# A head dealt out anew: decay tables made row by row, and jobs moved between VectorE, ScalarE and GpSimd

## The chip, the cores and the metric

The kernel runs on one core of a Trainium2 chip. The metric is the device time of one execution in microseconds (us). Engines are named as in the profile: PE is TensorE (PEld its weight loads), DVE is VectorE, ACT is ScalarE, POOL is GpSimd, SP is SyncE, which here only issues transfers.

## What is computed

A block of a network on 2048 tokens of 640 channels, all in float32. First a state-space convolution between a layer norm and a residual, then a gated product of two matrices between another layer norm and a residual; shift, scale and gate of both come from one small vector `c`.

```python
mod = (silu(c) @ w_mod).reshape(1, 6, 1, -1)
sa, ca, ga, sb, cb, gb = ...                         # six rows of 640
h = layernorm(x) * (1 + ca) + sa
# convolution: per channel d, kernel K[d, l] = Re sum_n C[d,n] * exp(dt*A[d,n]*l) * dt*B[d,n], 192 states, 2048 taps
x = x + ga * (irfft(rfft(h, 4096) * rfft(K, 4096))[:2048] + h * Dskip)
h = layernorm(x) * (1 + cb) + sb
x = x + gb * (((h @ w_gate) * (h @ w_up)) @ w_down)  # 640 -> 1536 -> 640
```

## The kernel before

**Stages.** The first part, called the head here, makes the convolution's kernel and does the convolution; the last part is the gated product, in which TensorE multiplies weights and activations split in a rounded and a residual half.

**The head.** The 640 channels are five blocks `db` of 128; each block is two halves `hf`, each half four steps `n`, so 40 steps in all. The kernel's powers exp(dt*A*l) are split in a phase (sine and cosine) and a decay. Long ones are products of short tables: an index l is made of a low part (8 values) and a high part (row). For each step POOL writes three outer products with `outer` (L649): the phase table `Ph` (`mk_ph`, 128x1536 int32), the decay `EQ` (`mk_eq`, 128x1536) and the decay `EP` (`mk_ep`, 128x768), the last two from a low table (`LQ`, `LP`) and a high one (`RH`). ACT makes sine and cosine of `Ph` into PSUM (`k_sin`, `k_cos`, `u_abs`), DVE multiplies them with `EQ` and `EP` (`k_mul`, L731, six instructions of a step), TensorE contracts the products (`kg_ma`, `kg_mb`, L745 and L760). `EP` and `EQ` have two buffers each. `kg_out` and `u_k` bring the result through a copy into the first Fourier stage.

The low and high decay tables come from `u_seeds(db)`, a list of small steps. Its step `s_r` (L521, L523) multiplies a seed in PSUM by row factors held in a tile `mults`, 3 rows into `RL` and 11 into `RH`; `s_e` takes exponentials on ACT: seven into `LP` (scale 64 l), one over all of `RH`, one over three rows of `RL`. For later blocks, both halves go in one `s_e`; `s_r` runs once for each half.

Beside this the convolution's input goes through its own stages: layer norm (`u_stats`, `u_hm`), first transform (`u_pre`), second stage (`u_g`), product in the frequency domain (`u_c`), back (`u_d`). Each of them ends with copies from PSUM to SBUF, by the helper `act` (L135, all ACT instructions bear this line). The last block's product is done in two parts of each quarter.

**The order** is written out. `SCHED` gives to each step of each job a number, thousands for a tick and the rest for the order within a tick; `at` files the steps, `due` runs them tick by tick, 0 to 433. Negative numbers come before. Every engine takes its instructions in this order. `SLOT` gives to each allocation its buffer by a letter. Steps at tick 433 (`hd`) are the beginning of the gated product: sums of up and gate weights (`sums_u`, L1004 to L1007, on POOL), rounded and residual halves (`hilo`: ACT rounds, DVE subtracts, L992), transposes of tokens (`tokens2`). Ahead of that stand the layer norm of the first tokens (`u_ln`), their transposes (`u_first`, residual at L1149), and the first products (`u_gate`, L1162). `raw_u` issues the loads of gate and up weights of one column block.

Of the kernel before, what the change touches and what calls it, by code (L numbers as in the profile page):

```python
# [32 lines left out]
    ml=(13002, -99000, 0),  # L33
    mr=(((20003, 22002), (17004, 17008)), ((6001, 13000), (14000, 14001)), ((1, 1000), (1001, 3001))),
    st=((3000, 3004), (-90000, -89999), (-100997, 3005), (9000, 11005), (9001, 11004), (12001, 15001), (21001, 25006), (7000, 11000), (11001, 12002), (-100998, 11002), (20001, 22000), (19001, 20004), (9002, 11003), (-101000, -89998), (17003, 17009), (15000, 19002)),
    hm=((23000, 24000), (13001, 41000), (-100999, 20010), (30000, 32006), (40003, 40004), (-98999, 30004), (30001, 32002), (29000, 38001), (40002, 43000), (38002, 47000), (56004, 68000), (21002, 44003), (79003, 86004), (61002, 69000), (77000, 85000), (61000, 84002)),
    rstd=(17005, 30003),
    tab=(91000, 121003),
    fo=(22003, 31003, 31005, 35001),
    e0=(-87000,),  # L40
    mc=((31004, 39005, 40006, 43001, 52000), (34000, 53002, 60000, 62000, 69002), (58000, 91004, 92001)),
    q=((22004, 32000, 39001, 40005, 42006, 44000, 44001, 44002, 51000, 51001, 56001, 56002, 57000, 57002), (66002, 89000, 95003, 101000, 107000, 107001, 111000, 112000, 123000, 123003, 124001, 131000, 131003, 131004), (137001, 175000, 176001, 186009, 188001, 189001, 197003, 197004, 201000, 201001, 203002, 204001, 204002, 206001), (210002, 226000, 252005, 264003, 265002, 268001, 268002, 268003, 268005, 272001, 275000, 277000, 280002, 281001)),
# [10 lines left out]
    hl=((397000, 389000), (385000, 381000)),  # L53
    ln=((400000, 412000, 412003), (401000, 419002, 427000, 431007, 431010)),
    hd=(433000, 433017, 433028, 433035, 433027, 433001, 433005, 433003, 433008, 433009, 433010, 433012, 433007, 433024, 433021, 433016, 433026, 433014, 433018, 433013, 433004, 433023, 433022, 433034, 433036, 433025, 433019, 433031, 433039, 433011, 433002, 433006, 433029, 433033, 433038, 433030, 433040, 433037, 433020, 433032, 433042, 433041, 433015, 4880, 4880),
    ru=(409003, 367001),
    hg=(428002, 428003, 431004, 431005, 431012),
    rt=(410000,),
)

SLOT = dict(
    pa='23402424034345',
    Kt='abaaabaaabaabbabbaabbb',
    Ph='abababababababababababababababababababab',
    PtA='babababababaabbaaaabaabababababababababa',
    TV='ababbaabbaaaabababaabaabbababbbaba',
    W='abbaababaabaabbaababa',
    f16='abababab',
# [61 lines left out]
def tile_kernel(ctx: ExitStack, tc: tile.TileContext, I, out):  # L130
# [1240 lines left out]
    def s_one(k):  # L1371
        hilo(*part(1, k - 2), AT[TV1 + k])
# [252 lines left out]
```

## Time and profile before

| what | value |
|---|---|
| median of three runs | 962.99 us (959.34 to 963.2) |
| the profiled execution | 962.99 us, span 961.2 us |
| busy in the span: PE, DVE, ACT, POOL | 864.6, 760.1, 569.7, 567.8 us |
| granted TensorE clock, mean | 0.975 of full speed |
| POOL's last table of the head ends | 421.9 us |
| last matmul of the 40 steps ends | 433.5 us |

In the tables that follow, a row of the table by stage gives busy time and, in brackets, the number of instructions for each engine; a row of a group gives line, engine, operation, output and inputs, shape and count, then busy time and mean nanoseconds of one, then the engine's idle time just before and what ended it. A row of one line gives shortest, median and longest duration in nanoseconds. A row of waits gives who waited for whom: total, times, longest. A row of the chain or the timeline starts with the time from the span's start and the length.

### The profile page before, as it was taken

What the parts mean: (1) busy time and instruction counts of PE and PEld (TensorE: products, weight loads), DVE (VectorE), ACT (ScalarE), POOL (GpSimd) and SP (SyncE); (2) the same over time, 40 slices, a digit from 0 to 9 for tenths busy, and PEclk for the clock granted to TensorE, in tenths of its full rate; (3) what the DMA queues carried; (4) which work ended last, traced back from release to release, by engine and by line L of the source; (5) the groups of instructions that cost most, each with busy time, mean ns of one, the idle gap of its engine ahead of it and who ended that gap; (6) DMA issues with size and microseconds to landing.
All of it is one profiled execution on the core that took longest, in us unless ns stands there. A gap on an engine that the chain in (4) does not pass through costs nothing.

```text
span 961.2 us, 26424 instructions
## 1 busy us (share of the span) xinstructions
PE 864.6 (90%) x11070; PEld 715.9 (74%) x11070; DVE 760.1 (79%) x1328; ACT 569.7 (59%) x1022; POOL 567.8 (59%) x419
## 2 busy tenths in 40 slices
PE   2778876898798699989889999999999999999998
PEld 1565655676575467678567888899998888889998
DVE  8988678888989988897899877696677877688452
ACT  6889988887987888864773322235555322224330
POOL 5999999799799999950126767631031544451000
PEclk9977999899999889999999999999999999999999
DMA  9487565444565644558953454255536222212241
GB/s 301 152 267 263 150 217 191 134 132 126 145 181 147 186 130 144 161 175 266 254 168 89 130 192 139 80 192 164 193 137 219 84 83 82 83 55 83 83 165 55
DMA packets 141320, 148.94 MB, mean 155 GB/s; under 512 B 8208, under 2 KB 119568, under 8 KB 139792
## 3 DMA queue, kind: packets, MB, share of 16 engines
q1 hardware_dynamic: 139904, 145.80, 48.6%
q8 instruction: 87, 1.43, 0.6%
q10 hardware_dynamic: 1296, 1.44, 0.5%
q14 instruction: 33, 0.27, 0.1%
HBM read 108.36 MB, written 38.86 MB: 153 GB/s over the span
## 4 chain that ended last, share of the span: by engine, by line
PE 49%; DVE 4%; ACT 1%; DMA 1%; issue 1%; DVEq 0%; SPq 0%; ACTq 0%
PE pa L1028 28%; PE pa L1455 17%; PE psg L1028 1%; DMA wga<-B_w_gate 1%; DVE sl L992 1%; PE psg L1108 0%; PE psg L1455 0%; DVE a L1147 0%; PE psg L1162 0%; DVE xb L1468 0%; ACT wsgh L135 0%; PE psfa L887 0%; DVE f16a L873 0%; DVE f16a L874 0%; PE psfb L887 0%
## 5 line engine op out<-in xcount | busy, mean ns | idle before, releaser
L649 POOL TENSOR_TENSOR EQ<-LQ,RH 128x1536 f32<-128x1536 f32 x40 | 124.2, 3106 | 2.2 <-DVE QtB L731 2.1
L135 ACT ACTIVATE z<-pa 128x512 f32<-128x512 f32 x24 | 14.4, 599 | 168.0 <-PE pa L1028 115.0
L992 DVE TENSOR_TENSOR wsgl<-wga,wsgh 128x640 fp32r<-128x640 f32 x72 | 69.8, 973 | 45.6 <-ACT wsgh L135 45.6
L135 ACT ACTIVATE wsgh<-wga 128x640 fp32r<-128x640 f32 x72 | 52.3, 732 | 63.4 <-PE pa L1455 34.1
L1399 POOL TENSOR_TENSOR z<-z,s 128x512 f32<-128x512 f32 x24 | 34.2, 1423 | 88.4 <-DVE s L1398 88.4
L1004 POOL TENSOR_TENSOR tf<-wur,wgb 128x256 f32<-128x256 f32 x24 | 18.8, 784 | 97.0 <-DVE wtl L992 58.9
L649 POOL TENSOR_TENSOR EP<-LP,RH 128x768 f32<-128x768 f32 x40 | 65.7, 1651 | 11.8 <-DVE PtB L731 11.8
L1455 PE MATMUL pa<-wsgh,sh 128*128 128x384 f32 (+1 forms) x295 | 68.6, 311 | 0.0
L1455 PE MATMUL pa<-wsgl,sh 128*128 128x384 f32 (+1 forms) x295 | 68.2, 310 | 0.0
L1455 PE MATMUL pa<-wsgh,sl 128*128 128x384 f32 (+1 forms) x295 | 68.2, 310 | 0.0
L649 POOL TENSOR_TENSOR Pha<-LH,DH 128x1536 int32<-128x1536 int32 (+1 forms) x21 | 62.4, 2971 | 1.8 <-ACT tra L135 1.6
L649 POOL TENSOR_TENSOR Phb<-LH,DH 128x1536 int32<-128x1536 int32 x20 | 62.3, 3113 | 0.0
L992 DVE TENSOR_TENSOR wtl<-tf,wth 128x256 fp32r<-128x256 f32 (+1 forms) x72 | 58.8, 844 | 0.0
L731 DVE TENSOR_TENSOR QtA<-tra,EQ 128x1024 f32<-128x1024 f32 x44 | 51.9, 1215 | 7.7 <-ACT tra L135 4.8
L1397 DVE TENSOR_TENSOR s<-pa,s 128x512 f32<-128x512 f32 x24 | 16.6, 690 | 42.8 <-PE pa L1028 37.8
L731 DVE TENSOR_TENSOR QtA<-trb,EQ 128x1024 f32<-128x1024 f32 x36 | 42.7, 1217 | 9.7 <-ACT trb L135 5.5
L760 PE MATMUL kg<-QtB,PtB 64*32 64x64 f32 x2560 | 46.1, 222 | 4.7 <-issue 2.7
L760 PEld LDWEIGHTS kg<-QtB,PtB 64*32 64x32 f32 x2560 | 39.1, 110 | 12.5 <-issue 6.4
L1028 PE MATMUL pa<-sh,wtl 128*128 128x512 f32 x144 | 44.7, 391 | 0.8 <-DVE wtl L992 0.8
L1455 PEld LDWEIGHTS pa<-wsgh,sl 128*128 128x128 f32 x295 | 45.3, 188 | 0.0
L1455 PEld LDWEIGHTS pa<-wsgl,sh 128*128 128x128 f32 x295 | 45.3, 188 | 0.0
L1455 PEld LDWEIGHTS pa<-wsgh,sh 128*128 128x128 f32 x295 | 45.3, 188 | 0.0
(653 smaller groups left out, 2854.7 us busy)
## 6 DMA issues: line engine op xcount, KB each, us to landing
wga<-wdg SPq DMA_DIRECT2D x24, 640.0 KB, 4.2
wga<-B_w_gate SPq DMA_DIRECT2D x12, 640.0 KB, 5.8
wgb<-B_w_gate SPq DMA_DIRECT2D x24, 320.0 KB, 3.3
wur<-B_w_up SPq DMA_DIRECT2D x24, 320.0 KB, 4.0
xb<-x2d SPq DMA_DIRECT2D x6, 1280.0 KB, 7.1
t_ti<-w_mod SPq DMA_DIRECT2D x3, 1600.0 KB, 9.5
t_tw<-w_mod SPq DMA_DIRECT2D x3, 1600.0 KB, 9.8
WD<-Wa SPq DMA_DIRECT2D x8, 512.0 KB, 4.1
```

Source lines behind the costliest of these rows:

```text
L135: return S.activation(o, i, f, **kw)
L649: G.tensor_tensor(o.rearrange("p x (h l) -> p x h l", l=8), lo.unsqueeze(2).to_broadcast([P, rows, nh, 8]), hi.rearrange("p h x -> p x h") ...
L731: V.tensor_tensor(t, tr, e.unsqueeze(1).to_broadcast([P, 2, R, 32]), op=OP.mult)
L760: PE.matmul(kg[j * 32 : j * 32 + 32, dd, :], PtB[lo : lo + 64, c, r, :], QtB[lo : lo + 64, c, r, :], start=False, stop=dd == 7 and c == 1, ...
L992: V.tensor_tensor(lo, v, hi, op=OP.subtract)
L1004: G.tensor_tensor(t[:, 0:2], u[:, 0:2], g[:, 0:2], op=OP.subtract)
L1028: PE.matmul(ps, w[a][:, k], x[b][:, l], start=n == 0 and m == 0, stop=n == 2 and m == len(ks) - 1)
L1397: V.tensor_tensor(S67[i], ps, S6[i], op=OP.add)
L1399: G.tensor_tensor(ZT[i], ZT[i], S67[i], op=OP.add)
L1455: PE.matmul(ACC[tb][t][c], x[:, ts], w[:, cs], start=st, stop=f == NF - 1 and n == 2 and (one or t % 2 == 1))
```

## The change

1. `s_r` becomes a copy of the seed into row 0 of `RL`, for one half (`r`, `R`, in block 0) or both at once (`S`, later blocks). `mults` is gone. `s_e` makes every row of `RH` and `RL` by one ACT exponential with the row's factor as its scale: three rows, seven rows, three rows, beside the seven of `LP`. Row 3 of `RH`, which is always 1, is set once.
2. Copies, scalings and two-operand instructions of the head go through `put` and `tt`, which look up an engine in a new table `ENG` by the job's key; without an entry the engine is that of before.
3. `SCHED` and `SLOT` have new numbers throughout: every job of the head has a new place. Among them: the loads of the first gate and up weights (`ru`) move from tick 409 to 426, the load of the gate row (`w`, second entry) from 431 to 370, the third `split_g` (`w`, fifth entry) from tick 380 to 409.
4. SBUF layout: `mults` (14 columns) goes and `ry` grows from 24 to 48 columns on the left side, `RH` is placed ahead of `LP`, and a tile `gap` of 24 columns is added on the right.

The diff, cut to its core:

```diff
 SCHED = dict(
...
-    q=((22004, 32000, 39001, 40005, 42006, 44000, 44001, 44002, 51000, 51001, 56001, 56002, 57000, 57002), ...
+    q=((22002, 28000, 38003, 43002, 44001, 50001, 50005, 54000, 54001, 54003, 55005, 58000, 59000), ...
...
-    w=(366001, 431008, 380000, 382001, 380001, 382000),
+    w=(366002, 370000, 382001, 389000, 409001, 387001),
...
-    ru=(409003, 367001),
+    ru=(426000, 391002),
...
+ENG = {('ep', 1): 'V', ('k', 1): 'V', ('ko', 5): 'V', ('pg', 1): 'V', ('pre', 0, 1, 1): 'V', ('k', 3): 'V', ('ep', 8): 'V', ('k', 4): 'V', ('ep', 10): 'V', ('pre', 0, 2, 0): 'V', ('ep', 9): 'V', ('ep', 11): 'V', ('ko', 11): 'V', ('pre', 1, 3, 1): 'V', ('g', 0, 2, 0): 'V', ('ep', 15): 'V', ('pre', 1, 1, 1): 'V', ('g', 0, 0, 0): 'V', ('c', 0, 3, 0): 'V', ('g', 1, 3, 0): 'V', ('c', 0, 0, 1): 'V', ('c', 0, 2, 1): 'V', ('g', 1, 2, 1): 'V', ('pre', 2, 3, 1): 'V', ('c', 1, 2, 0): 'V', ('c', 1, 2, 1): 'V', ('g', 1, 0, 1): 'V', ('ep', 25): 'V', ('c', 1, 0, 1): 'V', ('g', 2, 0, 0): 'V', ('g', 2, 0, 1): 'V', ('ko', 29): 'V', ('ep', 30): 'V', ('c', 2, 2, 1): 'V', ('pre', 3, 3, 0): 'V', ('ep', 33): 'V', ('c', 2, 3, 0): 'V', ('c', 2, 3, 1): 'V', ('ep', 34): 'V', ('k', 30): 'V', ('k', 28): 'V', ('c', 3, 0, 1): 'V', ('ko', 39): 'V', ('c', 3, 3, 0): 'V', ('g', 4, 0, 0): 'V', ('k', 38): 'V', ('lg', 2): 'G', ('lg', 3): 'G', ('lg', 1): 'G', ('k', 39): 'V', ('hn', 2, 0): 'G', ('hn', 0, 1): 'A', ('hn', 1, 2): 'G', ('ft', 1): 'A', ('fl', 1): 'G', ('hn', 4, 0): 'G', ('hn', 4, 1): 'A', ('hn', 4, 2): 'G', ('hn', 4, 3): 'A', ('fl', 2): 'G', ('hn', 3, 2): 'G', ('hn', 3, 3): 'A', ('hi', 1, 2): 'G', ('hi', 1, 3): 'A', ('su', 0, 2): 'V', ('su', 0, 3): 'V', ('lu', 0, 4): 'G', ('su', 2, 0): 'V', ('su', 2, 2): 'V'}
-SEG = ("l", "a", "b", "c", "ud", "D", "r", "R", "x", "E", "f", "g", "h", "v")
+SEG = ("l", "a", "b", "c", "ud", "D", "S", "x", "E", "f", "g", "h", "v")
...
+    def put(k, o, i, d="A", **kw):
+
+        e = ENG.get(k, d)
+        if e == "A":
+            act(o, i, AF.Identity if kw else AF.Copy, **kw)
+        elif kw:
+            (V if e == "V" else G).tensor_scalar(o, i, kw["scale"], kw["bias"], op0=OP.mult, op1=OP.add)
+        else:
+            V.tensor_copy(o, i)
+
+    def tt(k, o, a, b, op, d="V"):
+
+        e = ENG.get(k, d)
+        (V if e == "V" else G).tensor_tensor(o, a, b, op=op)
+
...
-    mults = const.tile([P, 14], F32, name="mults")
-    for k, m in enumerate((1536, 1024, 512, 0, 8, 16, 24, 32, 40, 48, 56, 1, 2, 4)):
-        V.memset(mults[:, k : k + 1], float(m))
...
-    ry = const.tile([P, 24], F32, name="ry")
+    ry = const.tile([P, 48], F32, name="ry")
...
+    RH = pk1.tile([P, 3, 11, 96], F32, name="RH")
     V.memset(LP[:, :, :, 0], 1.0)
-    RH = pk1.tile([P, 3, 11, 96], F32, name="RH")
+    V.memset(RH[:, :, 3], 1.0)
...
         def s_r(h):
-            ps = T["ps"]
-            free(h, "ep", "eq", "lq")
-            V.tensor_tensor(g4(Rl[h])[:, 0:3], ps[:, 0, hs[h]].unsqueeze(1).to_broadcast([P, 3, 4, 24]),
-                            mults[:, 11:14].unsqueeze(2).unsqueeze(3).to_broadcast([P, 3, 4, 24]), op=OP.mult)
-            V.tensor_tensor(g4(Rh[h]), ps[:, 0, hs[h]].unsqueeze(1).to_broadcast([P, 11, 4, 24]),
-                            mults[:, 0:11].unsqueeze(2).unsqueeze(3).to_broadcast([P, 11, 4, 24]), op=OP.mult)
+            for i in h:
+                free(i, "lq")
+            rl = RL[:, 0:2, 0].rearrange("p h (s r) -> p h s r", r=24)[:, h[0] : h[-1] + 1]
+            V.tensor_copy(rl, T["ps"][:, 0, hs[h[0]].start : hs[h[-1]].stop].rearrange("p (h s) r -> p h s r", s=4))
...
             for l in range(1, 8):
                 act(lp[:, :, :, l], rl[:, :, 0], AF.Exp, scale=64.0 * l)
-            act(rh, rh, AF.Exp)
-            act(rl[:, :, 0:3], rl[:, :, 0:3], AF.Exp)
+            for k in (2, 1, 0):
+                act(rh[:, :, k], rl[:, :, 0], AF.Exp, scale=512.0 * (3 - k))
+            for k in range(4, 11):
+                act(rh[:, :, k], rl[:, :, 0], AF.Exp, scale=8.0 * (k - 3))
+            for k in (2, 1, 0):
+                act(rl[:, :, k], rl[:, :, 0], AF.Exp, scale=float(2**k))
...
-        outer(EP[n % 2], LP[:, hf % 3, r], RH[:, hf % 3, 3::-1, r], 24, 4, OP.mult)
+        outer(EP[n % 2], LP[:, hf % 3, r], RH[:, hf % 3, 3::-1, r], 24, 4, OP.mult, ("ep", n))
...
-            act(Ft, r[c])
+            put(("pre", db, q, c), Ft, r[c])
...
-    def hilo(hi, lo, v):
+    def hilo(hi, lo, v, k=None):
         act(hi, v)
-        V.tensor_tensor(lo, v, hi, op=OP.subtract)
+        tt(k, lo, v, hi, OP.subtract)
...
```

In `ENG`, V is DVE, A is ACT and G is POOL. Keys: `ep` an EP table, `pg` a multiplication of `u_pre` in block 0 (L798), `k` the copy of `u_k`, `ko` that of `kg_out`, `pre`, `g`, `c` the copies of these stages (block, quarter, which one), `lg` the residue of a gate weight block, `fl` and `ft` residue and scaling in `u_first`, `hn` and `hi` the normalisation of the first tokens, `su` the sums of up weights and `lu` the residues of these.

More of the change, by code (lines that the diff above doesn't have):

```diff
@@ L37 @@
[L37 to L42, printed above, removed]
@@ L59 @@
+    hg=(421001, 425000, 425003, 429000, 429002),
+    rt=(379001,),
 )
 SLOT = dict(
-    pa='23402424034345',
-    Kt='abaaabaaabaabbabbaabbb',
+    pa='54335403423235',
+    Kt='abaaabaaabaaababbaabaa',
     Ph='abababababababababababababababababababab',
-    PtA='babababababaabbaaaabaabababababababababa',
-    TV='ababbaabbaaaabababaabaabbababbbaba',
-    W='abbaababaabaabbaababa',
+    PtA='abbabaaaabababbbaabababababababababababa',
+    TV='ababbaabababbaaabbbababaababbbbabb',
+    W='ababbaabaabababaababa',
@@ L409, in u_hm @@
         need(1, "rs", q < 6)
-        act(x, x, AF.Identity, scale=rs1[:, q : q + 1], bias=nm1[:, q : q + 1])
+        put(("hm", q), x, x, scale=rs1[:, q : q + 1], bias=nm1[:, q : q + 1])
         SY.dma_start(hm[:, q, :], x)
@@ L441, in u_seeds @@
         Dh, Dl = ([R[(2 * db + h) % len(R)] for h in range(2)] for R in (DH, DL))
-        Rh, Rl = ([R[:, (2 * db + h) % R.shape[1]] for h in range(2)] for R in (RH, RL))
+        Rl = [RL[:, h] for h in range(2)]
         def halves(R, hh):
@@ L535, in s_e @@
         def s_e(*hh):
+            for h in hh:
+                free(h, "ep", "eq")
             lp, rh, rl = (halves(R, hh) for R in (LP, RH, RL))
@@ L591, in u_seeds @@
         one = lambda f, *a: lambda: f(*a)
-        steps = dict(l=s_l, a=s_a, b=s_b, c=s_c, d=one(s_d, 0), D=one(s_d, 1), r=one(s_r, 0), R=one(s_r, 1), u=s_u, x=s_x,
+        steps = dict(l=s_l, a=s_a, b=s_b, c=s_c, d=one(s_d, 0), D=one(s_d, 1), r=one(s_r, (0,)), R=one(s_r, (1,)), S=one(s_r, (0, 1)), u=s_u, x=s_x,
                      e=one(s_e, 0), E=one(s_e, 0, 1), f=s_f, G=s_G, g=s_g, h=s_h, v=s_v)
@@ L645, in tab_eq, with outer @@
         double(LQ, (rl[:, 1], rl[:, 2]), OP.mult)
-    def outer(o, lo, hi, rows, nh, op):
-        G.tensor_tensor(o.rearrange("p x (h l) -> p x h l", l=8),
-                        lo.unsqueeze(2).to_broadcast([P, rows, nh, 8]),
-                        hi.rearrange("p h x -> p x h").unsqueeze(3).to_broadcast([P, rows, nh, 8]), op=op)
+    def outer(o, lo, hi, rows, nh, op, k=None):
+        tt(k, o.rearrange("p x (h l) -> p x h l", l=8),
+           lo.unsqueeze(2).to_broadcast([P, rows, nh, 8]),
+           hi.rearrange("p h x -> p x h").unsqueeze(3).to_broadcast([P, rows, nh, 8]), op, "G")
     def mk_ph(n, a=None):
@@ L847, in u_g @@
         H = Gt.rearrange("p (c i) d -> p c i d", c=2)
-        act(H[:, 0], ph[0])
-        act(H[:, 1], ph[1])
+        for c in range(2):
+            put(("g", db, qd, c), H[:, c], ph[c])
         GH[db, qd] = H
@@ L927, in u_d @@
             Vt = ring(fp, [P, 2, 4, P], "gh" if c < 2 else "TV")
-            act(Vt[:, 0], r[0])
-            if c:
-                act(Vt[:, 1], r[1])
-            else:
-                V.tensor_copy(Vt[:, 1], r[1])
+            for t in range(2):
+                put(("d", c, t), Vt[:, t], r[t], "A" if c or t == 0 else "V")
         yield
@@ L1015, in split_u @@
         if "a" in parts:
-            hilo(*(w[:, 2:4] for w in WT[i]), t[:, 2:4])
+            hilo(*(w[:, 2:4] for w in WT[i]), t[:, 2:4], ("lu", i, 0))
         if "b" in parts:
-            hilo(*(w[:, 0:2] for w in WT[i]), t[:, 0:2])
-            hilo(*(w[:, 0:3] for w in WU[i]), u[:, 2:5])
+            hilo(*(w[:, 0:2] for w in WT[i]), t[:, 0:2], ("lu", i, 1))
+            hilo(*(w[:, 0:3] for w in WU[i]), u[:, 2:5], ("lu", i, 2))
         if "c" in parts:
-            hilo(*(w[:, 4:8] for w in WT[i]), t[:, 4:8])
-            hilo(*(w[:, 3] for w in WU[i]), g[:, 4])
+            hilo(*(w[:, 4:8] for w in WT[i]), t[:, 4:8], ("lu", i, 3))
+            hilo(*(w[:, 3] for w in WU[i]), g[:, 4], ("lu", i, 4))
     def prod(ps, ks):
@@ L1028, in prod @@
                 PE.matmul(ps, w[a][:, k], x[b][:, l], start=n == 0 and m == 0, stop=n == 2 and m == len(ks) - 1)
-    BANK, PRE = [0], [True]
+    BANK = [0]
     def pa(j=None, side=False):
@@ L1088, in head_n @@
             x = XB[tb][:, i, k * P : k * P + P]
-            if i % 2:
-                G.tensor_scalar(hn[:, i, :], x, rs[:, i : i + 1], nm[:, i : i + 1], op0=OP.mult, op1=OP.add)
-            else:
-                act(hn[:, i, :], x, AF.Identity, scale=rs[:, i : i + 1], bias=nm[:, i : i + 1])
+            put(("hn", k, i), hn[:, i, :], x, "AG"[i % 2], scale=rs[:, i : i + 1], bias=nm[:, i : i + 1])
         return hn
@@ L1099, in head_i @@
             x = XB[tb][:, i, :]
-            act(x, x, AF.Identity, scale=rs[:, i : i + 1], bias=nm[:, i : i + 1])
+            put(("hi", tb, i), x, x, "G" if tb == 1 and i == 3 else "A", scale=rs[:, i : i + 1], bias=nm[:, i : i + 1])
     def a_tile(j):
@@ L1108, in head_t @@
             PE.transpose(ps[:, i * P : i * P + P], hn[:, i], ident)
-        if dve:
-            V.tensor_scalar(tv, ps, cbT[:, k : k + 1], sbT[:, k : k + 1], op0=OP.mult, op1=OP.add)
-        else:
-            act(tv, ps, AF.Identity, scale=cbT[:, k : k + 1], bias=sbT[:, k : k + 1])
+        put(("tv", k) if PRE[0] else None, tv, ps, "V" if dve else "A", scale=cbT[:, k : k + 1], bias=sbT[:, k : k + 1])
     def u_ln(tb):
@@ L1144, in u_first @@
         hi, lo = (h[:, k] for h in HX[0])
-        act(hi, ps, AF.Identity, scale=cbT[:, k : k + 1], bias=sbT[:, k : k + 1])
+        put(("fh", k), hi, ps, scale=cbT[:, k : k + 1], bias=sbT[:, k : k + 1])
         tv = a_tile(TV0 + k)
-        V.tensor_scalar(tv, ps, cbT[:, k : k + 1], sbT[:, k : k + 1], op0=OP.mult, op1=OP.add)
+        put(("ft", k), tv, ps, "V", scale=cbT[:, k : k + 1], bias=sbT[:, k : k + 1])
         yield
-        V.tensor_tensor(lo, tv, hi, op=OP.subtract)
+        tt(("fl", k), lo, tv, hi, OP.subtract)
         mark("t0", k)
@@ L1336, in tile_kernel @@
                             + [("tf", [P, 8, P], F32, 1), ("wth", [P, 8, P], F32R, 2), ("wtl", [P, 8, P], F32R, 2), ("wsuh", [P, 4, P], F32R, 2),
-                               ("wsul", [P, 4, P], F32R, 2)] + [(f"a{j}", [P, 512], F32, 1) for j in (*range(5), *range(15, 24))]):
+                               ("wsul", [P, 4, P], F32R, 2)] + [(f"a{j}", [P, 512], F32, 1) for j in (*range(5), *range(15, 24))] + [("gap", [P, 24], F32, 1)]):
         FIRST[n] = gp.tile(sh_, dt_, name=n, bufs=b_)
@@ L1357, in s_sums @@
         s4 = tmp(TMP[1 + k])
-        V.tensor_tensor(s1, u(k), u(k + 2), op=OP.add)
-        V.tensor_tensor(s2, s1, t(k), op=OP.subtract)
-        E = V if PRE[0] else G
-        E.tensor_tensor(s3, t(k), u(k), op=OP.subtract)
-        E.tensor_tensor(s4, t(k + 2), s2, op=OP.subtract)
+        for j, v in enumerate(((s1, u(k), u(k + 2), OP.add), (s2, s1, t(k), OP.subtract), (s3, t(k), u(k), OP.subtract), (s4, t(k + 2), s2, OP.subtract))):
+            tt(("ss", k, j) if PRE[0] else None, *v, "V" if j < 2 or PRE[0] else "G")
         for j, v in enumerate((s1, s2, s3, s4)):
@@ L1368, in s_split @@
     def s_split(k, j):
-        hilo(*part(2, 2 * j - 2 + k), SV.pop((j, k)))
+        hilo(*part(2, 2 * j - 2 + k), SV.pop((j, k)), ("ls", k, j) if PRE[0] else None)
     def s_one(k):
-        hilo(*part(1, k - 2), AT[TV1 + k])
+        hilo(*part(1, k - 2), AT[TV1 + k], ("lo", k) if PRE[0] else None)
     def s_five():
         d5 = tmp(TMP[0])
-        (V if PRE[0] else G).tensor_tensor(d5, AT[TV0 + 4], AT[TV1 + 4], op=OP.subtract)
-        hilo(*part(2, 8), d5)
+        tt(("s5", 0) if PRE[0] else None, d5, AT[TV0 + 4], AT[TV1 + 4], OP.subtract, "V" if PRE[0] else "G")
+        hilo(*part(2, 8), d5, ("s5", 1) if PRE[0] else None)
     ZT, S6, S67 = {}, {}, {}
```

76 lines of the change are left out of this document (40 added, 36 removed).

## The prediction

> **What bounds the kernel now.** I read the page's busy totals first, then the table by stage, then the chain that ended last, then POOL's waits.
>
> ```profile
> PE 864.6 (90%) x11070; PEld 715.9 (74%) x11070; DVE 760.1 (79%) x1328; ACT 569.7 (59%) x1022; POOL 567.8 (59%) x419
> ```
>
> TensorE at 90% is an average over unlike stages, so I cut the span where the bound changes: at POOL's first large table, at POOL's last one, at the last kernel-generating matmul, and where TensorE stops waiting.
>
> ```profile
> core 0: us, PE busy (x) PEld busy (x) DVE busy (x) ACT busy (x) POOL busy (x), PEclk, DMA share, GB/s
> 0.00:14.40 14.40, 2.32 (x12) 1.60 (x12) 12.12 (x70) 9.04 (x19) 3.55 (x13) 1.00 0.85 242
> 14.40:421.93 407.53, 335.94 (x7490) 253.07 (x7492) 350.64 (x568) 347.18 (x602) 383.49 (x235) 0.94 0.57 174
> 421.93:433.50 11.57, 11.02 (x328) 9.73 (x330) 10.94 (x16) 5.27 (x10) 0.00 (x0) 1.00 0.85 258
> 433.50:507.40 73.90, 65.40 (x841) 50.22 (x841) 63.18 (x162) 48.61 (x85) 12.05 (x19) 1.00 0.74 218
> 507.40:961.20 453.80, 449.88 (x2407) 401.26 (x2407) 323.27 (x515) 159.59 (x308) 168.68 (x154) 1.00 0.38 122
> ```
>
> In the second row (the table stage, 407.5 us) POOL is busy 383.5 us, 94%: it is the bound, with 24.0 us of idle. DVE has 56.9 us of idle, ACT 60.3. In the two rows behind it (the transition, 85.5 us) DVE is busiest, 74.1 us. In the last row TensorE is busy 449.9 of 453.8 us; nothing that the change touches can shorten that. The chain, in order of time, agrees:
>
> ```profile
> 442.38 2.21 ACT wsgh L135 x4
> ...
> 445.52 1.55 DVE wsgl L992 x2
> ...
> 507.43 124.95 PE pa L1028 x549
> ```
>
> Up to 507.4 the chain runs mostly over DVE and ACT, from there over TensorE alone. So the change acts on the first 507.4 us only. POOL's idle time in the table stage has one large cause:
>
> ```profile
> POOL EP L649 <- DVE PtB L731: 11.8, 3, 6.1
> POOL LQ L643 <- DVE RL L571: 2.3, 3, 1.1
> ```
>
> POOL may not write the next EP table before DVE has read the one two steps back (three waits, 11.8 us).
>
> **The change, part by part.** *Decay tables.* Before, DVE multiplies the seed by the row factors (L521, L523, once for each of ten halves) and ACT takes one wide exponential; after, DVE copies the seed and ACT makes each row with the factor as its scale.
>
> ```profile
> L523 DVE TENSOR_TENSOR RH<-psfa,mults 128x1056 f32<-128x1056 f32 x6 | 7.5, 1246 | 0.0
> L521 DVE TENSOR_TENSOR RL<-psfa,mults 128x288 f32<-128x288 f32 x6 | 2.7, 446 | 0.0
> L571 DVE COPY RL<-psfa 128x96 f32<-128x96 f32 x4 | 0.8, 252 | 2.8 <-PE psfa L460 2.8
> L135 ACT ACTIVATE RH<-RH 128x2112 f32<-128x2112 f32 x4 | 7.9, 1964 | 0.0
> L135 ACT ACTIVATE RH<-RH 128x1056 f32<-128x1056 f32 x2 | 2.2, 1082 | 0.0
> L135 ACT ACTIVATE RL<-RL 128x576 f32<-128x576 f32 x4 | 2.7, 663 | 0.0
> L135 ACT ACTIVATE RL<-RL 128x288 f32<-128x288 f32 x2 | 0.9, 426 | 0.0
> L135 ACT ACTIVATE ptb<-ptb 128x192 f32<-128x192 f32 x10 | 3.6, 360 | 0.8 <-DVE ptb L490 0.7
> L135 ACT ACTIVATE RL<-trb 128x96 f32<-128x96 f32 x2 | 0.4, 248 | 3.1 <-PE trb L460 3.1
> ```
>
> DVE sheds 10 x (1.246 + 0.446) = 16.9 us (the four calls in other buffers last as long) and gains two copies of 96 at 0.25 and four of 192, estimated at 0.36: 1.9. Net -15.0, of which 1.4 lies in the first 14.4 us. ACT sheds 7.9 + 2.2 + 2.7 + 0.9 = 13.7 and gains 13 rows per call: 4 x 13 x 0.360 + 2 x 13 x 0.248 = 25.2. Net +11.5, which ACT's 60.3 us of idle covers; uncovered, each of the four later calls would hold up the sines behind it by 13 x 0.360 - 2.63 = 2.1 us. In the opening the copy saves DVE 1.4 us and the 13 rows cost ACT 13 x 0.248 - 1.51 = 1.7 us: +0.3, under the load of the phase table that POOL is doing then; I take zero.
>
> *Tables off POOL.* The new assignment gives DVE ten of the 40 EP tables and one of the four multiplications of L798.
>
> ```profile
> L649 POOL TENSOR_TENSOR EQ<-LQ,RH 128x1536 f32<-128x1536 f32 x40 | 124.2, 3106 | 2.2 <-DVE QtB L731 2.1
> L649 POOL TENSOR_TENSOR EP<-LP,RH 128x768 f32<-128x768 f32 x40 | 65.7, 1651 | 11.8 <-DVE PtB L731 11.8
> L798 POOL TENSOR_TENSOR hfa<-hfa,f16a 128x512 f32<-128x512 f32 x2 | 2.6, 1280 | 0.0
> L731 DVE TENSOR_TENSOR QtA<-tra,EQ 128x1024 f32<-128x1024 f32 x44 | 51.9, 1215 | 7.7 <-ACT tra L135 4.8 <-POOL EP L649 1.9 <-issue 0.7
> L731 DVE TENSOR_TENSOR QtB<-tra,EQ 128x512 f32<-128x512 f32 x44 | 28.6, 681 | 0.7 <-ACT tra L135 0.7
> ```
>
> POOL sheds 10 x 1.65 + 1.28 = 17.8 us: 383.5 becomes 365.7. On DVE an EP of 768 elements lies midway between 512 at 0.681 and 1024 at 1.215: 0.95. Ten and the multiplication make 10.2 us. That isn't all, because the existing L731 products read one operand from PSUM, and these eleven read both from SBUF. Such instructions, while POOL works too, look like this (the first row from 510 to 620 us, the second from 640 to 700 us, where POOL is mostly idle; then four rows of the timeline):
>
> ```profile
> L992 DVE TENSOR_TENSOR wsgl<-wga,wsgh x8: 811/1124/1824, 511.5 to 587.8; 128x640 fp32r<-128x640 f32 x8
> L992 DVE TENSOR_TENSOR wsgl<-wga,wsgh x18: 816/822/1356, 642.0 to 698.3; 128x640 fp32r<-128x640 f32 x18
> 487.10 0.73 POOL L1006 TENSOR_TENSOR tf<-wur 128x256 f32<-128x256 f32 x1
> 487.21 1.17 DVE L1149 TENSOR_TENSOR hl<-a,hh 128x512 fp32r<-128x512 f32 x1
> 487.79 1.18 POOL L1007 TENSOR_TENSOR tf<-wgb,tf 128x256 f32<-128x256 f32 x1
> 488.90 0.68 DVE L1149 TENSOR_TENSOR hl<-a,hh 128x512 fp32r<-128x512 f32 x1
> ```
>
> The same subtraction takes 0.68 us alone and 1.17 when it starts inside a POOL instruction; POOL's next one then takes 1.18 instead of 0.73. They take turns. So each of the eleven waits for the POOL instruction under way, from 0 to one EQ of 3.1 us; I take half, 1.55, so 17.1 us on DVE at full price, and POOL is held for their own 10.2 us. POOL's load is then 375.9 us, bounded below by 365.7 if nothing collides. The Trainium skill, "SBUF — State Buffer", section "Who interferes with whom", states this as a rule: a DVE instruction with two SBUF inputs contends with a GpSimd instruction that reads SBUF, and the second one blocks until the first ends. The rows above agree (1.17 against 0.68), and the rule speaks against this part of the change: by it the table stage sheds 7.6 us of POOL load, and without it 17.8.
>
> *Copies off ACT.* 36 copies of a PSUM bank go from ACT to DVE, all but about three in the table stage.
>
> ```profile
> L135 ACT ACTIVATE f16a<-psfb 128x512 f32<-128x512 f32 x10 | 5.8, 595 | 0.9 <-PE psfb L827 0.7 <-PE psfb L782 0.3
> L932 DVE COPY gha<-psfa x1: 692/692/692, 468.1 to 468.1; 128x512 f32<-128x512 f32 x1
> ```
>
> ACT: 33 x 0.595 = -19.6. DVE: 33 x 0.692 = +22.8. They read PSUM, so they don't collide with POOL. Loads of the stage: ACT 347.2 + 11.5 - 19.6 = 339.1. DVE 350.6 + 22.8 + 10.2 - 13.6 = 370.0 without waits for POOL and 387.1 with all of them. PE keeps its 335.9. POOL 375.9 plus the 24.0 us of idle of now gives a stage of 399.9 us: **-7.6**. I don't count the 11.8 us of EP waits as saved: an EP on DVE stands in order behind its reader and can't wait for it, but DVE is fuller, so I expect late DVE products in its place. ScalarE's table loads stay as many, since sine, root, exponential and arctangent alternate as often in both orders.
>
> *Transition.* Three of the four first weight residues (L992, the wsgl of 445.52 above, two of them in 1.55 us) go to POOL, which stands idle there: 3 x 0.77 = -2.3 on the chain. Two of the five L1149 residues go to POOL, one scaling of L1147 to ACT, and two of four L1004 sums to DVE; one copy of the last Fourier stage comes to DVE. On the far engine each is slower or no faster; I count the four together at -0.6. The row of gate factors is loaded earlier, ahead of the last loads on SP's queue instead of behind them; nobody waits for it. The load of the first up-weights is issued later, behind the transposes of the last two u_first columns (below at 484.21) instead of before those of the first.
>
> ```profile
> 484.21 0.60 PE psfc L1141 x4
> ...
> wur<-B_w_up SPq DMA_DIRECT2D x24, 320.0 KB, 4.0
> 485.58 0.74 POOL L1004 TENSOR_TENSOR tf<-wur,wgb 128x256 f32<-128x256 f32 x1
> ```
>
> Its reader starts at 485.58; issued near 484 and landing in 4.0 us it would come at 488, 2.4 us late, and two of the four sums on DVE give back 2 x 0.74. What waits is ACT's rounding and DVE's residue of these sums, second in the order at 433, with the other rounding and residue work behind them. I count 0, and up to +2.4. Sum of the transition: **-2.9**, between -6 and +2.
>
> *Order and layout.* That every job has a new place moves no work by itself, SP's loads and stores included; its effect is in how much idle time is left, so it is in the range, from 10 us less to 10 us more of POOL idle time. The 14 row factors and their memsets go, one memset of a constant row comes, a small tile grows, another is added on the right, and RH and LP swap. Cost 0. The cover is the last stage's 0.38 DMA share; and EQ, written to two buffers, shows one duration, so the place of a tile isn't seen there.
>
> **Sum.** -7.6 - 2.9 = -10.5 us. The profiled execution took 963.0 us (span 961.2 and 1.8 around it) and is itself the median of the three. 963.0 - 10.5 = **952.5**.
>
> **Rivals.** *(A) No collision to speak of:* the eleven DVE instructions fall into POOL's gaps. POOL sheds 17.8, the transition 2.9: 942.3. For it: POOL waits 24 us anyway. Against: it is busy 94% of the stage. *(B) The idle time eats it:* POOL has less to do but waits longer for DVE, as in the three EP waits; the stage stays, and only the transition gains: 960.1. For it: four engines lie between 336 and 387 us, closer together than now. *(C) DVE becomes the bound, slower:* with all its waits for POOL DVE carries 387.1 us. Its idle time now is 56.9, nearly all of it waiting for ACT, PE and POOL. The stage is longer than 407.5 once more than 20.4 of it stays; the whole is over 0.5% slower once more than 28 stays. If 35 stay, the stage is 422.1, +14.6, and with the transition 974.7. For it: an in-order DVE queue hands each wait for POOL on to the products behind it. Against: a wait for POOL partly replaces a wait for ACT.
>
> **How the numbers follow.** 0.5% is 4.8 us, about what a measurement of this kernel can tell from no change: faster is under 958.2, slower over 967.8. Chances: forecast 0.50, A 0.15, B 0.20, C 0.15. Faster is forecast and A, 0.65; same is B, 0.20; slower is C, 0.15. The forecast's own range is 946 to 958 (transition bounds and a few us of idle); the range that leaves out 2 in 10 runs from A to the near edge of C, 940 to 969.
>
> **What would show it.** POOL busy in the table stage near 376 us; ten DVE EP tables, each 0.95 us or more, several over 2; EQ or phase tables on POOL lasting about 0.9 longer beside them; ACT near 339 us; the stage near 400 us; the last stage unchanged at 453.8. The forecast is wrong if POOL's idle time grows by over 7 us, if EP on DVE takes 0.95 everywhere (then A), if DVE's idle time stays over 20 us (then B or C), or if the last stage moves.

## The result, and the profile after

The changed kernel takes 955.58 us, the median of six runs (953.56 to 956.96); the kernel before takes 962.35 on the same chip. The ratio is 0.9927, with a 95% interval of 0.9911 to 0.9944: faster by 6.8 us, where 10.5 were forecast. The profiled execution has a span of 955.2 us, 6.0 less than the one before.

The table by stage of the changed kernel is cut at POOL's first large table, at POOL's last one, at 433.50 us again, and where TensorE stops waiting. The cut at 433.50 is a mere moment: in the kernel before, the last product of the 40 steps ends at 435.5 us and not at 433.5, as the texts ahead have it, and in the changed kernel it starts at 432.4. So the two rows of the transition are read as one.

```profile
core 0: us, PE busy (x) PEld busy (x) DVE busy (x) ACT busy (x) POOL busy (x), PEclk, DMA share, GB/s
0.00:14.29 14.29, 2.32 (x12) 1.60 (x12) 11.98 (x57) 9.01 (x21) 3.52 (x13) 1.00 0.85 263
14.29:418.71 404.42, 338.10 (x7488) 257.36 (x7490) 369.09 (x596) 339.45 (x636) 372.80 (x224) 0.94 0.56 173
418.71:433.50 14.79, 12.98 (x400) 11.09 (x398) 11.84 (x18) 5.29 (x10) 0.00 (x0) 1.00 0.87 286
433.50:503.60 70.10, 63.74 (x770) 49.41 (x770) 62.64 (x162) 46.23 (x80) 18.70 (x24) 1.00 0.72 220
503.60:955.20 451.60, 447.43 (x2407) 398.33 (x2407) 322.83 (x516) 158.87 (x308) 166.77 (x152) 1.00 0.37 123
```

The table stage lost 3.1 us (404.42 against 407.53), the transition 0.6 (418.71 to 503.60, 84.9, against 85.5), and the last stage 2.2 (451.60 against 453.80), the one that was not to change. These are single executions. With the same order and engines, in the three kernels below that differ from the changed one only in the place of tiles (and a few constants set at the start), POOL's last table ends between 416.7 and 418.6 us and the transition lasts 84.8 to 87.0; in the two that so differ from the kernel before, 421.2 to 422.2 and 85.5. So the table stage gained some 3 to 5 us, and a gain in the transition isn't clear of the scatter. In the table stage POOL shed 10.7 us of load (372.80 against 383.49), but its idle time went from 24.0 to 31.6. POOL's waits there show with what:

```profile
POOL Phb L153 <- ACT trb L136: 8.3, 4, 4.7
POOL EP L153 <- DVE PtB L751: 6.4, 2, 4.0
POOL Pha L153 <- ACT trb L136: 3.8, 1, 3.8
POOL hfa L153 <- PE kg L780: 3.2, 1, 3.2
```

The waits for DVE to release EP went from 11.8 to 6.4 us; in their place stand 12.1 us of waits until ACT has read a phase table. The longest of them, in the timeline:

```profile
161.93 2.71 ACT L136 ACTIVATE LP<-RL 128x192 f32<-128x192 f32 x7
164.41 2.64 ACT L136 ACTIVATE RH<-RL 128x192 f32<-128x192 f32 x10
166.96 1.00 ACT L136 ACTIVATE RL<-RL 128x192 f32<-128x192 f32 x3
167.97 1.28 ACT L136 ACT_TABLE_LOAD   x1
169.27 0.60 ACT L136 ACTIVATE trb<-Phb 128x512 f32<-128x512 int32 x1
170.01 3.11 POOL L153 TENSOR_TENSOR Phb<-LH,DH 128x1536 int32<-128x1536 int32 x1 [4.75 <-ACT trb L136]
```

The sine that reads the phase table stands behind a burst of 20 exponentials and a table load, and POOL stands idle for 4.75 us until it has been read.

The EP tables, and the one on DVE that collided hardest:

```profile
L153 POOL TENSOR_TENSOR EP<-LP,RH x30: 1639/1652/2386, 15.9 to 414.0; 128x768 f32<-128x768 f32 x30
L153 DVE TENSOR_TENSOR EP<-LP,RH x10: 948/1157/3923, 22.9 to 370.8; 128x768 f32<-128x768 f32 x10
109.37 3.14 POOL L153 TENSOR_TENSOR Phb<-LH,DH 128x1536 int32<-128x1536 int32 x1
109.40 3.92 DVE L153 TENSOR_TENSOR EP<-LP,RH 128x768 f32<-128x768 f32 x1
112.44 3.84 POOL L153 TENSOR_TENSOR EQ<-LQ,RH 128x1536 f32<-128x1536 f32 x1
```

The DVE table was issued 0.03 us after a POOL table had begun. It waited for POOL's end at 112.5 and ended at 113.3; POOL's next table lasted 3.84 instead of 3.11. This one stretched to 3.92; the shortest, with no wait, took 0.95.

### The profile page after: what moved, and what is told of

It is laid out like the page before. It is cut to its first block, busy times and chain, and to the rows that moved or that the text cites. A ratio compares the mean times of both kernels' runs of the same rounds, so it can differ in the third digit from the quotient of the medians.

```text
span 955.2 us, 26459 instructions
## 1 busy us (share of the span) xinstructions
PE 864.6 (91%) x11070; PEld 717.8 (75%) x11070; DVE 778.4 (81%) x1345; ACT 558.9 (59%) x1052; POOL 561.8 (59%) x411
## 4 chain that ended last, share of the span: by engine, by line
PE 61%; DVE 16%; ACT 11%; DMA 5%; issue 5%; SPq 1%; POOL 0%; DVEq 0%; ACTq 0%; POOLq 0%
PE pa L1045 28%; PE pa L1462 15%; DVE QtA L751 3%; ACT trb L136 2%; PE kg L765 2%; ACT tra L136 1%; PE kg L780 1%; PE psfb L847 1%; PE psg L1045 1%; DVE QtB L751 1%; DMA x2d<-xsb 1%; PE psfa L847 1%; PE psfc L847 1%; PE psfb L300 1%; DVE EP L153 1%
## 5 line engine op out<-in xcount | busy, mean ns | idle before, releaser
L153 POOL TENSOR_TENSOR EP<-LP,RH 128x768 f32<-128x768 f32 x30 | 50.3, 1678 | 6.4 <-DVE PtB L751 6.4
L751 DVE TENSOR_TENSOR QtA<-tra,EQ 128x1024 f32<-128x1024 f32 x40 | 47.5, 1215 | 5.5 <-ACT tra L136 3.8
L751 DVE TENSOR_TENSOR QtA<-trb,EQ 128x1024 f32<-128x1024 f32 x40 | 47.2, 1217 | 2.2 <-ACT trb L136 1.2
```

The source lines that it names most:

```text
L153: (V if e == "V" else G).tensor_tensor(o, a, b, op=op)
L751: V.tensor_tensor(t, tr, e.unsqueeze(1).to_broadcast([P, 2, R, 32]), op=OP.mult)
```

## The experiments

Each ratio compares with the kernel before on the same chip; the changed kernel's is 0.9927. Differences in us from the changed kernel are taken between medians on different chips; worked out from the ratios they come out up to 1.9 us larger. Stages are read from one execution of each kernel. A passage set off tells what was expected of the run.

### The last stage: the place of tiles

**Right side alone**, in the kernel before:

```diff
-... for j in (*range(5), *range(15, 24))]):
+... for j in (*range(5), *range(15, 24))] + [("gap", [P, 24], F32, 1)]):
```

> The kernel before with the small tile on the right side (24 columns) as its only edit, so that every other tile on that side starts at another address. Theory (the place of the right-hand tiles sets the pace of the down products): the 24 matmuls of one step of L1455 go from 3.52 us to 3.47, their 384-column ones from 340 ns to 331, the stage from 507 us on gets 2.2 us shorter, 962.4 becomes about 960. Rival (the shorter last stage of the changed kernel has another cause): no pace changes, 962.4.

**Right side undone**, in the changed kernel:

```diff
-... + [("gap", [P, 24], F32, 1)]):
+...):
```

> The changed kernel without that small tile. Theory (right-hand placement): the step of 24 matmuls goes back from 3.47 to 3.52 us, 340 ns for 384 columns, 955.6 becomes about 958. Rival: 955.6 and 331 ns stay.

**Left side undone**, in the changed kernel:

```diff
+    mults = const.tile([P, 14], F32, name="mults")     # with its 14 memsets
-    ry = const.tile([P, 48], F32, name="ry")
+    ry = const.tile([P, 24], F32, name="ry")
```

> The changed kernel with the left side's small constants as before (the 14 row factors kept, unused, and the small tile back to 24 columns), the right side as changed. Theory (only the right side counts): 955.6, 331 ns stays, up to 0.3 us for 14 memsets at the start. Rival (the left side counts, where the moving weights of the down products are): 340 ns and about 958.

**Both sides, nothing else**, in the kernel before: the right-hand tile as above, and on the left, where the 14 factors are still needed, `ry` at 32 columns, which gives the left side the same length as in the changed kernel if tiles are rounded up to 32 bytes (the helpers `put` and `tt` are there too, with `ENG` empty, and the one memset of `RH`):

```diff
-    ry = const.tile([P, 24], F32, name="ry")
+    ry = const.tile([P, 32], F32, name="ry")
+... + [("gap", [P, 24], F32, 1)]):
```

> The kernel before with both sides of the layout as changed and one memset more, all else as before: order, engines, wide decay tables. Theory (left and right place together set the pace of the last stage's products): a step of 24 down products 3.47 us and not 3.52, the 549 products of the first half 125.3 and not 125.0, the whole 2.2 us faster, 960. Rival (the pace of the changed kernel comes from its order): 3.52 us and 962.

**Right side 128 bytes further on**, in the changed kernel:

```diff
-("gap", [P, 24], F32, 1)
+("gap", [P, 56], F32, 1)
```

> The changed kernel with the added tile on the right at 56 columns in place of 24, so that the right side lies 128 bytes further on. Theory (what counts on the right is the address in steps of 128 bytes): 955.6, all paces as changed. Rival (steps of 256 bytes or finer count): the pace of a step of 24 down products moves away from 3.47 us, and the whole by 1 to 4 us either way.

What tells is the pace, from the chain in order of time of each kernel: the long stretch of 549 products with gate and up weights and that of 312 down products (those with `w_down`) of the first half (start, length, line, count), for before, changed, right alone, right undone, left undone, both alone, and right further on, in this order:

```profile
507.43 124.95 PE pa L1028 x549
636.46 45.76 PE pa L1455 x312
```

```profile
503.57 125.35 PE pa L1045 x549
633.01 44.89 PE pa L1462 x312
```

```profile
507.66 125.97 PE pa L1028 x549
637.71 45.77 PE pa L1455 x312
```

```profile
504.69 125.73 PE pa L1045 x549
634.51 45.54 PE pa L1462 x312
```

```profile
505.50 125.97 PE pa L1048 x549
635.55 45.77 PE pa L1465 x312
```

```profile
506.72 125.31 PE pa L1048 x549
636.12 44.89 PE pa L1465 x312
```

```profile
501.50 124.98 PE pa L1045 x549
630.56 45.76 PE pa L1462 x312
```

These rows carry the verdict, since they repeat to a few hundredths of a us: the changed kernel and the one with only the layout, whose orders and engines differ throughout the head, have 44.89 both; right alone and left undone, which have the same layout, have 125.97 and 45.77 both. So the pace belongs to the place of the tiles, and not to the order. The whole last stage says it again, at a granted clock of 1.00 in every one of these kernels: from the start of the 549 products to the end of the span it lasts 453.77 us before and 451.58 with both sides alone, against 451.63 in the changed kernel, and 455.84 and 455.90 with right alone and left undone. Neither side does it alone: with the right side alone the down products keep 45.77 and the others become slower, 1.0 us over 549; with the left side alone (right undone) they take 45.54, and the others 0.8 more. That theory of mine, that the right side sets the pace, falls. By the clock: right alone 964.25 us (ratio 1.0019, interval 1.0003 to 1.0034), right undone 959.09 (0.9964, 0.9950 to 0.9977), left undone 961.17 (0.9985, 0.9967 to 1.0003). Both alone take 960.83 us (0.9971, 0.9947 to 0.9995), 2.0 us less than before, with an interval of 0.5 to 5 us; the last stage of the profiles gives 2.2. That is the layout's part of the gain. With the right side 128 bytes further on the pace returns to that of before (124.98, 45.76), and the last stage to 453.60, so it isn't steps of 128 bytes that count, and that theory falls too; the whole stays within the noise of the changed kernel, 956.87 (0.9939, 0.9920 to 0.9958), and in its profiled execution a head 2.1 us shorter hides the longer last stage. Which operand of a matmul makes the difference is open. The down products that gain are among those of 384 columns with a residual half: the longest of a rounded weight with a residual activation takes 340 ns before and 331 after.

```profile
L1455 PE MATMUL pa<-wsgh,sl x84: 278/309/340, 643.6 to 679.9; 128*128 128x384 f32 x42, 128*128 128x256 f32 x42
L1462 PE MATMUL pa<-wsgh,sl x84: 279/305/331, 640.2 to 675.6; 128*128 128x384 f32 x42, 128*128 128x256 f32 x42
```

### The table stage: rows, EP tables, copies

**Decay tables row by row alone**, in the kernel before (its own order, engines and layout; the seed is copied once for each half, as that order has it):

```diff
-            V.tensor_tensor(g4(Rh[h]), ps[...]..., mults[:, 0:11]..., op=OP.mult)     # and the same into Rl
+            V.tensor_copy(rl, T["ps"][...])
-            act(rh, rh, AF.Exp)
+            for k in (2, 1, 0): act(rh[:, :, k], rl[:, :, 0], AF.Exp, scale=512.0 * (3 - k))     # and so on
```

> The kernel before with the decay tables row by row, in its own order and layout. DVE sheds 15 us of load, ACT takes 11.5 more. Theory (POOL bounds the table stage and its load is the same): 962 within 2 us. Rival 1 (ACT's longer bursts hold up the sines): up to 2.1 us for each of four later blocks, so up to 970. Rival 2 (POOL's 11.8 us of waits for late DVE products shrink with DVE's load): down to 957.

965.48 us (1.0027, 1.0008 to 1.0046): slower by some 3 us, a little more than the theory allowed. Its table stage:

```profile
14.40:426.17 411.77, 337.38 (x7488) 255.00 (x7490) 337.45 (x558) 353.13 (x666) 383.37 (x235) 0.95 0.56 172
```

DVE sheds 13.2 us (350.64 to 337.45) and ACT takes 6.0 more (347.18 to 353.13), with POOL's load unchanged; the stage is 4.2 us longer. So in the order of before 13.2 us less on DVE bring no gain, and rival 2 falls. Rival 1 has the sign, but POOL's waits don't show its path: the one for a sine to have read the phase table falls from 1.6 to 0.7 us, while POOL waits 5.2 us for DVE's copies of the amplitudes into row 3 of `RL`, against 2.3 before.

**Wide tables in the changed kernel**:

```diff
+            V.tensor_tensor(g4(Rh[h]), ps[...]..., mults[:, 0:11]..., op=OP.mult)     # and into Rl, for each half
-            for k in (2, 1, 0): act(rh[:, :, k], ...)     # and the other rows
+            act(rh, rh, AF.Exp)
+            act(rl[:, :, 0:3], rl[:, :, 0:3], AF.Exp)
...     # the 14 factors come back, with ry at 32 columns
```

> The changed kernel with the decay tables made as before (DVE multiplies the seed by the factors, ACT takes wide exponentials), order, layout of both sides and assignments as changed. DVE 369 to about 382 us in the table stage, ACT 339 to 328. Theory (DVE has 35 us of idle left and is late for POOL already): 3 to 8 us slower. Rival (ACT is what POOL waits for, and its bursts get 2 us shorter): faster by up to 4 us.

969.14 us (1.0075, 1.0050 to 1.0099), 13.6 slower than the changed kernel, more than the theory gave. Its table stage, and its waits of POOL:

```profile
14.29:433.20 418.91, 340.30 (x7504) 258.54 (x7504) 385.75 (x612) 334.82 (x573) 373.80 (x224) 0.93 0.55 168
POOL Phb L153 <- ACT trb L136: 11.1, 4, 5.6
POOL EQ L153 <- DVE QtB L754: 9.2, 6, 4.3
POOL EP L153 <- DVE PtB L754: 7.0, 2, 3.9
```

ACT carries 4.6 us less here and DVE 16.7 more, and the stage is 14.5 longer. POOL still waits longer for ACT (11.1 us against 8.3), and for DVE to release EQ (9.2; before this edit 2.2). So what hurts comes by way of DVE, and the row-by-row exponentials alone don't make the waits for ACT. The edit also puts the factor products where the order has only a short copy; this run doesn't part their place from their length.

**EP tables back on POOL**:

```diff
-ENG = {('ep', 1): 'V', ..., ('pg', 1): 'V', ...}
+ENG = {...}     # the ten ('ep', n) and ('pg', 1) taken out
```

> The changed kernel with the ten EP tables and the one multiplication of L798 back on POOL, all else as changed. Theory (POOL's load bounds the table stage; collisions cost 7 of the 17.8 us that it sheds): POOL in that stage from 372.8 to about 383, the whole 7 to 11 us slower, 963 to 967. Rival (the collisions and the fuller DVE eat what POOL sheds): within 2 us of 955.6.

965.00 us (1.0043, 1.0020 to 1.0065), 9.4 slower than the changed kernel, as the theory had it. Its table stage:

```profile
14.29:430.70 416.41, 338.49 (x7492) 256.68 (x7494) 355.91 (x585) 339.93 (x636) 383.65 (x235) 0.94 0.55 168
```

POOL is busy 10.9 us more than in the changed kernel and the stage is 12.0 longer, though DVE carries 13.2 less: the stage follows POOL's load here.

**Ten other EP tables on DVE**:

```diff
-('ep', n) for n in 1, 8, 9, 10, 11, 15, 25, 30, 33, 34
+('ep', n) for n in 4, 5, 13, 14, 18, 19, 22, 27, 36, 37
```

> The changed kernel with ten other EP tables on DVE (steps 4, 5, 13, 14, 18, 19, 22, 27, 36, 37 in place of 1, 8, 9, 10, 11, 15, 25, 30, 33, 34), all else the same. Theory (a DVE table that starts inside a POOL instruction waits for its end, and the ten of the change are placed where that seldom happens): mean duration of the ten goes from 1.45 us to 2 to 3, the whole 5 to 15 us slower. Rival (the place doesn't matter, loads are the same): 1.45 us and 955.6 within 2.

981.16 us (1.0200, 1.0173 to 1.0227). The same number of tables, and 25.6 us slower than the changed kernel:

```profile
L153 DVE TENSOR_TENSOR EP<-LP,RH x10: 947/2476/3339, 67.2 to 428.7; 128x768 f32<-128x768 f32 x10
14.29:443.48 429.19, 344.31 (x7502) 263.03 (x7504) 379.24 (x597) 340.25 (x637) 371.49 (x224) 0.93 0.53 163
```

The mean of one goes from 1.45 us to 2.32 (the median from 1.16 to 2.48), as the theory had it; the whole loses more than the theory gave. POOL's load is even a little lower (371.49), so the loss is idle time: DVE's load rose by 10.2 us, and POOL's idle time by 26.1 (429.19 - 371.49 = 57.7, against 31.6). The ten tables' own waiting is 8.6 us of the loss. The rest goes with where they stand in DVE's order and what waits for them there; this run doesn't split it.

**Copies back on ACT**:

```diff
-ENG = {..., ('k', 1): 'V', ('ko', 5): 'V', ('pre', 0, 1, 1): 'V', ...}
+ENG = {...}     # the 36 entries k, ko, pre, g, c taken out
```

> The changed kernel with the 36 copies of PSUM banks back on ACT: ACT 339 to about 360 us in the table stage, DVE 369 to 346. Theory (ACT was relieved because POOL waits for sines that have read the phase tables, 12.1 us in the changed kernel): 3 to 8 us slower, POOL's waits for ACT over 15 us. Rival (DVE, the second fullest engine, is the one that is late): 2 to 6 us faster.

983.39 us (1.0231, 1.0190 to 1.0271), 27.8 slower than the changed kernel: right in sign, far off in size. Its table stage:

```profile
14.29:433.00 418.71, 339.46 (x7492) 258.01 (x7494) 353.53 (x566) 353.70 (x668) 373.00 (x224) 0.93 0.55 168
```

ACT carries 14.3 us more, DVE 15.6 less, POOL the same, and the stage is 14.3 longer. POOL's waits for ACT to have read a phase table rise from 13.0 us to 21.1, as the theory had it. Another 6.2 us of this execution, whose span is 975.9 us, lie in the transition (91.0 against 84.9). No engine is over 90% busy in the table stage, and yet ACT's us cost about one us each.

**The order of before**, with the rows, the eleven DVE jobs, the copies and both sides of the layout as changed, the transition's assignments as before (the seed is copied once for each half, as that order has it):

```diff
-SCHED, SLOT, SEG of the changed kernel
+SCHED, SLOT, SEG of the kernel before
-ENG = {...}
+ENG = {...}     # without hn, hi, ft, fl, lg, su, lu
```

> The change without its new order: the order and the buffer letters of before, with the decay tables row by row, the ten EP tables and the multiplication on DVE, the 36 copies on DVE and both sides of the layout as changed; the transition's assignments stay as before. Theory (the order is fitted to where the work is; with the order of another assignment DVE's new work stands in the way): 963 to 980, slower than before in spite of the shorter last stage. Rival (the loads decide, the order only settles details): POOL sheds 10 us as in the changed kernel, 953 to 958.

1003.27 us (1.0426, 1.0385 to 1.0466): 40 us slower than before. Its table stage lasts 442.95 us with nearly the loads of the changed kernel (POOL 372.3, DVE 371.3, ACT 339.8), 38.5 longer. Turns between DVE and POOL aren't the reason, since the ten DVE tables take 1.39 us on average, no more than in the changed kernel. POOL waits 28.9 us for DVE to release EQ and EP:

```profile
POOL EQ L153 <- DVE QtB L751: 16.0, 5, 8.3
POOL EP L153 <- DVE PtB L751: 12.9, 3, 6.1
```

The assignment without the order loses six times what both together gain: the loads alone don't give the time. No run has the new order with every assignment as before, so what the order is worth by itself is not shown.

### The transition

**Assignments of the transition as before**, in the changed kernel:

```diff
-ENG = {..., ('lg', 2): 'G', ('hn', 2, 0): 'G', ('ft', 1): 'A', ('fl', 1): 'G', ('su', 0, 2): 'V', ('lu', 0, 4): 'G', ...}
+ENG = {...}     # lg, hn, hi, ft, fl, su, lu taken out
```

> The changed kernel with every assignment of the transition as before (three weight residues and two token residues on DVE, the up-weight sums on POOL, the normalisation as before), the table stage's assignments and the order as changed. Theory (the transition is bound by DVE): 1 to 3 us slower, 957 to 959. Rival (these residues weren't on the chain any more in the new order): 955.6 within 0.7.

959.33 us (0.9985, 0.9964 to 1.0005), 3.7 slower than the changed kernel, somewhat over the theory's range. The table stage ends where it did, and the transition shows the difference:

```profile
14.29:418.49 404.20, 336.19 (x7480) 257.56 (x7482) 368.42 (x595) 339.24 (x636) 372.29 (x224) 0.94 0.56 173
418.49:507.72 89.23, 79.15 (x1175) 62.20 (x1171) 78.23 (x185) 51.31 (x90) 11.43 (x19) 0.98 0.71 220
```

89.2 us against 84.9: the assignments are worth 4.3 us in the new order by these two executions, and 2 to 4 by the scatter of the transition above.

## Why the prediction was right or wrong

**What bounds what: right for POOL, but too narrow.** POOL's load counts: 10.9 us more of it made the stage 12.0 longer (EP tables back on POOL). So does ACT's, which has 65 us of idle in the stage: 14.3 us more made it 14.3 longer (copies back on ACT). The chain that ended last puts the changed kernel's head mostly on TensorE, DVE and ACT; with the EP tables back POOL has a part in it. The shares of the span, by engine, for the changed kernel and for that one:

```profile
PE 61%; DVE 16%; ACT 11%; DMA 5%; issue 5%; SPq 1%; POOL 0%; DVEq 0%; ACTq 0%; POOLq 0%
PE 58%; DVE 16%; ACT 9%; POOL 7%; issue 5%; DMA 4%; SPq 1%; DVEq 0%; ACTq 0%; POOLq 0%
```

The chain of before that the prediction reads begins at 431.5 us, so it couldn't agree with a bound in the table stage. And in the transition TensorE was the busiest engine and not DVE: 11.02 + 65.40 = 76.4 us against 74.1.

**POOL's load: right, its parts less so.** 375.9 us were forecast, 372.8 came. The eleven DVE jobs were to hold POOL for their own 10.2 us; they held it for 7.1 (372.8 against 365.7 with no collision).

**The wait of an EP table on DVE: too dear.** I took half an EQ, 1.55 us, for each. The ten take 1.45 us on average (14.5 us in all), so 0.5 of waiting each, and only one lasts over 2 us where I expected several. The step that failed is the assumption that they start at a random moment: the ten other tables wait 1.37 us on average, near my 1.55. The mechanism itself, turns between DVE and POOL when DVE reads both operands from SBUF, is shown by the row of 3.92 us; of the 80 DVE products `QtA`, which read one operand from PSUM, none lasts over 1.23.

**DVE and ACT: luck in both sums.** DVE came out at 369.1 us, forecast 370.0 without waits; but the eleven jobs are worth 13.2 us on it and not 10.2, and the copies 15.6 and not 22.8. ACT came out at 339.5, forecast 339.1, by two errors that cancel. The rows cost 6.0 us and not 11.5 (the run with the rows alone), because I multiplied counts by the mean duration, and instructions in a row overlap: the ten RH rows above take 2.64 us together, 0.26 each, though the mean of one is 0.36. The copies freed 14.3 and not 19.6; that this has the same reason is likely, and not shown.

**POOL's idle time: the step that cost most.** I kept it at 24.0 us; it is 31.6. The waits for DVE to release EP fell, and waits until ACT has read a phase table took their place; I had named late DVE products instead. So the stage gained 3.1 us and not 7.6: rival B in part. It wasn't bound by DVE as rival C had it, though DVE's idle time of 35.3 us is what that rival asked for: DVE's load stayed at 369.1 and not 387.1, since the waits for POOL were short. With the ten other tables, or with the wide tables, DVE was late and the stage longer than before.

**The transition: mis-sized.** 2.9 us forecast, 0.6 came, though the assignments are worth 4.3. The new order gave back the rest: with the assignments of before it takes 89.2 us, and the order of before takes 85.5. The late load of up-weights cost nothing visible: its reader on POOL starts at 480.50, earlier than the 485.58 of before.

**The layout: a step that failed.** I priced it at 0 from the equal durations of EQ, a POOL table; TensorE's operands were not considered. It is worth about 2 us of the 6.8. The texts ahead say that RH and LP change places; they don't, only the line that sets a constant of LP moved.

**The order.** I called it no work and gave it 10 us to either side. It is more: the assignments of the table stage in the order of before cost 40 us.

**The sum owes something to luck.** Of the 6.8 us some 2 come from the last stage, which the sum held unchanged and whose moving the prediction named as a sign against itself. Two more of these signs came: POOL's idle time grew by 7.6 us, over the 7 allowed, and DVE kept 35.3 us of idle, over the 20. So the collisions happen as described, but where the time was gained is right only in part.

## What to carry to other kernels

In a schedule written out by hand on in-order engines, price a moved instruction by where it lands as well as by its length: ten other tables of the same size cost 26 us. In the table stage of the changed kernel the fullest engine is busy 92%, and 14.3 us put on ACT, which had 65 us of idle, cost 14.3 us; so an engine's idle time isn't free room. Ask which queue each freed us stands in. For instructions issued in a row, take busy time divided by count, not the mean duration (0.26 against 0.36 us for a decay row).

## What the runs showed of the hardware

The place of tiles in SBUF changes TensorE's pace in these products. Each pair below gives the stretch of 549 products and that of 312 down products: 124.95 and 45.76 us as before (124.98 and 45.76 with the right side 128 bytes further on in the changed kernel), 125.97 and 45.77 with the right side alone, 125.73 and 45.54 with the left side alone, 125.35 and 44.89 with both. The same combination gave the same pace within 0.05 us in kernels of different order. The layout that is best for one group isn't best for the other: the changed kernel's gains 0.9 on the down products and loses 0.4 on the others. Why is open.

A DVE product with both operands in SBUF and a POOL product take turns: 0.95 us by itself, 3.92 when it was issued 0.03 us behind the start of a POOL instruction of 3.14, with POOL's next one at 3.84 and not 3.11.
